# Two-scale attention and two feed-forward layers: the local attention as forty bands of 64 keys, in pairs

## The chip, the cores and the metric

The kernel runs on one core of a Trainium2 chip. The metric is the device time of one execution in microseconds; smaller is better. Engines are named as in the profile: PE (TensorE matmul), PEld (its weight loads), DVE (VectorE), ACT (ScalarE), POOL (GpSimd), SP (SyncE, which issues the DMAs).

## What is computed

Inputs are q, k, v of shape (4, 8, 576, 64): 4 batches, 8 heads, 576 tokens, 64 values a head. All is float32.

```
q_d, k_d, v_d = means of four neighbouring tokens (144 each)
out_up    = repeat(softmax(q_d k_d^T / 8) v_d, 4)
scores    = where(|i - j| < 4, q k^T / 8, -1e9)
out_local = softmax(scores) v
x = (out_up + out_local) as 2304 tokens x 512
h = x @ w_in   (512 x 2048);  x = relu(h)^2 @ w_out   (2048 x 512)
h = x @ w_in2  (512 x 2048);  out = (h * cos(h)) @ w_out2
```

The local attention looks three tokens to either side. In 64 neighbouring tokens a query therefore needs at most 70 keys.

## The kernel before

**Local attention.** A task `window(w)` (L453) works off 64 queries of one batch with their 64 + 6 keys; there are 36 windows, nine a batch. Heads are held in pairs, 128 partitions = 2 heads x 64. For a window PE writes the mask (L478, two bf16 matmuls of 280 columns, in the windows before `W0[3]`; DVE adds it in the later ones, L499), then eight score products (L488, one head each: contraction over 64 partitions, 64 queries x 70 keys, plain float32, all into one PSUM bank). The two heads of a pair use the lower left and the upper right 64 x 64 corner of the array. A softmax follows (`exps`, L359: maximum L360, exponential on ACT L365 or subtraction L372 and L376, sum L378, reciprocal L506, division L507), four transposes (L517, one for each head pair, 70 keys become 70 partitions), a copy out of PSUM on ACT (L519), and eight V products (L537: contraction over 70 keys, 64 x 64). DVE adds the coarse attention (L553) into `xt`, ACT rounds it to `xh` (L564), DVE takes the rest `xl` (L565). In the trace each plain float32 matmul is two MATMUL records.

**Coarse attention.** `pool(b)` (L229) sums four tokens; `down(b, hp)` (L380) is its attention: scores L391, transposes L412, V product L428.

**Feed-forward 1.** Its tokens go in five blocks of 512, 448, 448, 448, 448 (`WINS1`, windows of 64). For each of 16 slices f of the hidden size `stage_a` (L718, 12 matmuls) gives h, ACT makes gt and gh (L746, L747, L734), DVE gl (L740), and `stage_b1` (L800, 12 matmuls) sums into four banks. The weights of slice f come as raw 1 MB loads, and `conv1(f)` with `split` (L586) makes two parts of them: ACT L591, DVE L593, L596, L598, ACT L605 (`hi`), and two subtractions L613 (`loa`, `lob`), on POOL in the first stage and on DVE later.

**Feed-forward 2** (L750, L818) follows without attention.

**Order.** Everything before the first `stage_a` is the first stage (`early`): pooling, the coarse attention of batch 0, the windows of block 0 and `conv1` of slices 0 to 2. After it tasks are advanced once or twice an iteration; `start_at` sets the iteration in which a window, a pool or a conversion begins, `RANK` who goes first, and a scheduler places the instructions of each engine. While block j is multiplied, the windows of block j + 1 are worked off between its matmuls. `need` and `done` count buffers: three PSUM banks `a` serve scores, transposes and V products (in the first stage the banks of `h` and `acc` too).

Of the kernel before, what the change touches and what calls it, by code (L numbers as in the profile page):

```python
# [24 lines left out]
WQ = 64  # L25
WK = WQ + 2 * HALO
NWB = S // WQ
NW = B * NWB
KTOK = SD // 2
# [6 lines left out]
WINS1 = (8, 7, 7, 7, 7)  # L36
# [27 lines left out]
RANK = {"down": 0, "window": 1, "pool": 2, "conv1": 3, "conv2": 3}  # L64


def window_of(w):
    b, i = divmod(w, NWB)
    t0 = i * WQ
    k0, k1 = max(t0 - HALO, 0), min(t0 + WQ + HALO, S)  # L70
    return b, i, t0, k0, k1
# [3 lines left out]
def kernel(  # L75
# [28 lines left out]
    const_sb = const.tile([P, P + WK], F32, name="const_sb")  # L104
    nc.sync.dma_start(out=const_sb, in_=consts)
    ident = const_sb[:, :P]
    const_b = const.tile([P, P + WK], BF16, name="const_b")
# [5 lines left out]
    for t, v in zip(magic, (MAGIC, -MAGIC)):  # L113
# [7 lines left out]
    y_d = [dramp.tile([P, NK, n * WQ], F32, name=f"y_d{j}") for j, n in enumerate(WINS1)]  # L121

    caps = {
        "a": 3, "h": 1, "acc": 4, "qkw": 3, "vw": 3, "pr": 4, "pt": 2, "xt": 2, "qp": 1, "xd": 2, "vp": 1, "av": 3, "pl": 2, "raw": 2,
# [37 lines left out]
    kept = [spare.pop() for _ in range(W0[1] // 2 + 1)]  # L162
# [66 lines left out]
    def pool(b):  # L229
# [8 lines left out]
        for i, hp in parts:  # L238
# [17 lines left out]
            if not early[0]:  # L256
                yield
# [18 lines left out]
    def load_bands():  # L276
        for w in range(0, W0[1], 2):
            t = wp.tile([P, 2 * DM], F32R, tag=f"hi{kept.pop(0)}", name="vband").bitcast(F32)[:WK]
            bands[w], bands[w + 1] = t[:, :DM], t[:, DM:]
            nc.sync.dma_start(  # L280
                out=t.rearrange("p (w c) -> p w c", w=2), in_=win_v[w:w + 2].rearrange("w p c -> p w c")
            )
# [160 lines left out]
    xts = {}  # L443
    placed, added = [0], [0]
# [8 lines left out]
    def window(w):  # L453
        b, i, t0, k0, k1 = window_of(w)
        n, off = k1 - k0, HALO - (t0 - k0)
        apart = early[0]
        if not apart:
            yield from need("qkw")
            qk = cm.tile([P, HPAIR * (WQ + WK)], F32, tag="qkw", name="qkw", bufs=caps["qkw"])
            nc.sync.dma_start(out=qk, in_=win_qk[w])  # L460
            qw = qk[:, :HPAIR * WQ].rearrange("p (h m) -> p h m", h=HPAIR)
            kw = qk[:, HPAIR * WQ:].rearrange("p (h s) -> p h s", h=HPAIR)
        if not apart:
            yield from need("vw")
            vw = cm.tile([WK, DM], F32, tag="vw", name="vw", bufs=caps["vw"])
# [45 lines left out]
        if not early[0]:  # L511
            yield
# [687 lines left out]
```

## Time and profile before

| | us |
|---|---|
| median of 3 runs | 932.44 (931.36 to 932.68) |
| profiled execution | 931.8 |
| its span, first to last instruction | 930.0 |
| PE busy in the span | 907.4 (98%) |
| DVE / ACT / POOL busy | 645.6 / 578.9 / 102.6 |
| DMA bytes | 222.77 MB |

The span is 1.8 us shorter than the execution and both belong to the same run. A matmul of the profile is counted busy until its modelled end, and several lie over one another; so a price for a group of them is better read from where the group and its successor start than from the sum of their durations.

### The profile page before, as it was taken

What the parts mean: (1) busy time and instruction counts of PE and PEld (TensorE: products, weight loads), DVE (VectorE), ACT (ScalarE), POOL (GpSimd) and SP (SyncE); (2) the same over time, 40 slices, a digit from 0 to 9 for tenths busy, and PEclk for the clock granted to TensorE, in tenths of its full rate; (3) what the DMA queues carried; (4) which work ended last, traced back from release to release, by engine and by line L of the source; (5) the groups of instructions that cost most, each with busy time, mean ns of one, the idle gap of its engine ahead of it and who ended that gap; (6) DMA issues with size and microseconds to landing.
All of it is one profiled execution on the core that took longest, in us unless ns stands there. A gap on an engine that the chain in (4) does not pass through costs nothing.

```text
span 930.0 us, 17583 instructions
## 1 busy us (share of the span) xinstructions
PE 907.4 (98%) x6858; PEld 830.1 (89%) x6858; DVE 645.6 (69%) x1231; ACT 578.9 (62%) x1024; POOL 102.6 (11%) x79
## 2 busy tenths in 40 slices
PE   7789999999999999999999999999999999999997
PEld 5668777888889888889899999999999999999997
DVE  6998885663667535646521168879888888879786
ACT  4787774545555455555543377777777776777774
POOL 2111101033033332132110000000000000000000
PEclk9999999999999999999999999999999999999999
DMA  9788876856898677976897876555656666655672
GB/s 230 220 318 299 310 260 205 303 184 221 285 338 290 240 252 250 314 257 231 304 323 248 309 286 199 203 182 197 206 182 196 207 202 194 211 182 196 212 234 102
DMA packets 74223, 222.77 MB, mean 240 GB/s; under 512 B 8932, under 2 KB 14436, under 8 KB 69916
## 3 DMA queue, kind: packets, MB, share of 16 engines
q1 hardware_dynamic: 74140, 221.64, 70.9%
q8 instruction: 54, 0.88, 0.4%
q14 instruction: 29, 0.24, 0.1%
HBM read 180.72 MB, written 40.89 MB: 238 GB/s over the span
## 4 chain that ended last, share of the span: by engine, by line
PE 87%; DVE 6%; DMA 3%; ACT 2%; issue 1%; SPq 0%; POOL 0%; DVEq 0%; ACTq 0%; POOLq 0%
PE ps_h L757 22%; PE ps_h L722 19%; PE acc L805 19%; PE acc L829 18%; DMA pl<-in_pool_v_dram 2%; PE ps_a L537 1%; DMA pl<-in_pool_qk_dram 1%; PE ps_a L488 1%; PE ps_a L517 1%; PE ps_warm L942 1%; PE ps_a L391 1%; PE ps_a L428 1%; PE ps_a L412 1%; PE acc L827 1%; DVE mx L360 1%
## 5 line engine op out<-in xcount | busy, mean ns | idle before, releaser
L757 PE MATMUL ps_h<-x,w2hi 128*128 128x256 f32 x1152 | 159.9, 281 | 0.0
L757 PEld LDWEIGHTS ps_h<-x,w2hi 128*128 128x128 f32 x1152 | 146.6, 189 | 0.1
L829 PE MATMUL acc<-bl,gh 128*128 128x256 f32 x504 | 140.5, 280 | 0.0
L740 DVE TENSOR_TENSOR gl<-gt,gh 128x448 fp32r<-128x448 f32 (+1 forms) x80 | 56.3, 704 | 115.3 <-ACT gh L734 56.2
L722 PE MATMUL ps_h<-xh,w1hi 128*128 128x448 f32 (+1 forms) x320 | 121.4, 381 | 2.8 <-ACT gt L746 1.8
L805 PE MATMUL acc<-gl,w1hi 128*128 128x448 f32 (+1 forms) x320 | 120.8, 377 | 0.2 <-DVE gl L740 0.2
L722 PE MATMUL ps_h<-xl,w1hi 128*128 128x448 f32 (+1 forms) x320 | 119.6, 374 | 0.5 <-DVE xl L565 0.5
L746 ACT ACTIVATE gt<-ps_h 128x448 f32<-128x448 f32 (+1 forms) x80 | 44.2, 552 | 117.3 <-PE ps_h L722 117.0
L805 PE MATMUL acc<-gh,w1hi 128*128 128x448 f32 (+1 forms) x320 | 109.4, 379 | 2.6 <-ACT gh L734 2.6
L829 PEld LDWEIGHTS acc<-bl,gh 128*128 128x128 f32 x504 | 94.9, 188 | 0.0
L805 PE MATMUL acc<-gh,lo 128*128 128x448 f32 x256 | 94.4, 369 | 0.0
L797 DVE TENSOR_TENSOR gl<-g,gh 128x896 fp32r<-128x896 f32 x72 | 78.2, 1086 | 11.0 <-ACT gh L792 11.0
L765 ACT ACTIVATE u<-ps_h,quarter 128x512 f32<-128x512 f32 x72 | 49.4, 686 | 51.4 <-PE ps_h L757 51.2
L829 PE MATMUL acc<-w2hi,gh 128*128 128x256 f32 x288 | 80.9, 281 | 0.0
L829 PE MATMUL acc<-w2hi,gl 128*128 128x256 f32 x288 | 80.3, 281 | 0.0
L772 DVE SCALAR_TENSOR_TENSOR r<-u,ps_h 128x512 f32<-128x512 f32 x72 | 49.4, 687 | 40.2 <-ACT u L767 34.8
L792 ACT ACTIVATE gh<-g 128x896 fp32r<-128x896 f32 x72 | 68.1, 946 | 10.7 <-DVE g L790 10.6
L777 ACT ACTIVATE r<-r,half_pi 128x512 f32<-128x512 f32 x72 | 51.8, 720 | 33.8 <-DVE r L773 33.8
L722 PEld LDWEIGHTS ps_h<-xh,w1hi 128*128 128x128 f32 x320 | 60.1, 188 | 12.0 <-ACT gt L746 3.4
L757 PE MATMUL ps_h<-x,w2lo 128*128 128x256 f32 x432 | 68.7, 281 | 0.0
L805 PEld LDWEIGHTS acc<-gh,w1hi 128*128 128x128 f32 x320 | 59.6, 188 | 10.2 <-ACT gh L734 3.1
L805 PEld LDWEIGHTS acc<-gl,w1hi 128*128 128x128 f32 x320 | 60.7, 190 | 7.0 <-DVE gl L740 0.5
(149 smaller groups left out, 1952.1 us busy)
## 6 DMA issues: line engine op xcount, KB each, us to landing
bl<-wo_d SPq DMA_DIRECT2D x70, 896.0 KB
raw<-in_w_dram SPq DMA_DIRECT2D x32, 1024.0 KB
lo<-lo_d SPq DMA_DIRECT2D x128, 256.0 KB
qkw<-in_win_qk_dram SPq DMA_DIRECT2D x28, 268.0 KB
pl<-in_pool_qk_dram SPq DMA_DIRECT2D x24, 288.0 KB
wo_d<-raw SPq DMA_DIRECT2D x16, 384.0 KB
out_dram<-o SPq DMA_DIRECT2D x18, 256.0 KB
lo_d<-loa SPq DMA_DIRECT2D x16, 256.0 KB
```

Of the source, the lines that this page charges most:

```text
L360: last["max"] = nc.vector.tensor_reduce(out=mx[:, 0], in_=sv, op=ALU.max, axis=AX.X).ins
L722: nc.tensor.matmul(h[:, :n], a[:, c * P:(c + 1) * P], x[:, c, :n], start=i == 0, stop=i == len(order) - 1)
L740: last["gl"] = nc.vector.tensor_tensor(out=gl, in0=gt, in1=gh.bitcast(F32), op=ALU.subtract).ins
L746: last["relu"] = nc.scalar.activation(out=gt, in_=h, func=AF.Relu).ins
L757: nc.tensor.matmul(h[:, s * TB:(s + 1) * TB], a[:, c * P:(c + 1) * P], x[:, c], start=i == 0, stop=i == len(order) - 1,)
L765: nc.scalar.activation(out=u, in_=h, func=AF.Identity, bias=quarter, scale=float(1.0 / (2 * math.pi)))
L772: nc.vector.scalar_tensor_tensor(out=r, in0=u, scalar=-PI2_HI, in1=hv, op0=ALU.mult, op1=ALU.add)
L777: nc.scalar.activation(out=r, in_=r, func=AF.Sin, bias=half_pi, scale=1.0)
L792: nc.scalar.activation(out=gh, in_=g[:, 1:], func=AF.Copy)
L797: nc.vector.tensor_tensor(out=gl, in0=g[:, 1:], in1=gh.bitcast(F32), op=ALU.subtract)
L805: nc.tensor.matmul(acc[d][:, :n], a, x, start=f == 0 and i == 0, stop=f == NF - 1 and i == 2)
L829: nc.tensor.matmul(o, a[:, x], b, start=opens and i == 0, stop=p == NP2 - 1 and i == 2 and (k % 2 == 1 or k == NPROD - 1),)
```

## The change

The 576 tokens of a batch are cut into ten bands of 60, 56 or 58 queries (`WIDTHS`) whose keys are exactly 64. There are 40 bands, eight in each block, and the blocks have 460, 460, 464, 460 and 460 tokens. A task `pair(q)` takes two bands. Scores and V products are 64 x 64 in every dimension: contraction over 64 partitions, 64 stationary columns, 64 (V: 56 to 60) moving columns. The four products that stand next to one another in the source have the four combinations of the lower or upper 64 rows with the left or right 64 columns of the array, and the two row halves write to two different PSUM banks. The order of the products follows: the query half `a` of a head pair picks the rows and the bank, the head pair's index `c` the output partitions; in the V products the key half `g` picks the rows and the bank. One softmax runs for each bank (`soft`), so two for a pair. A transposed piece now has 128 x 128, two for each bank. Masks are written for each corner. The adds of the coarse part are two for a pair.

Beside that: `conv1(0)` holds its three DVE steps back until all first-stage divisions are issued, `conv1(1)` until the first block's input is complete; the first-stage subtractions L613 move from POOL to DVE; `pt` has 5 buffers instead of 2, `qkw` and `vw` 2 larger ones instead of 3; pairs start by a changed table of iterations; `pool` of the last two batches loads one step more slowly.

```
-WQ = 64
-WK = WQ + 2 * HALO
-NWB = S // WQ
+WQ = WK = 64
+WIDTHS = (60, 56, 58, 58, 56, 56, 58, 58, 56, 60)
+NWB = len(WIDTHS)
...
-WINS1 = (8, 7, 7, 7, 7)
+WINS1 = (8,) * 5
...
+    def soft(s, sv, pr_tag, pr, q, a, pts):
...
+        yield from exps(s, sv, mx, pr, SCALE, a == 0 if apart else 2 * q < W0[2])
...
+        for i in range(2):
+            both_g = pr[:, 2 * i:2 * i + 2].rearrange("p g s -> p (g s)")
+            last["pe"] = nc.tensor.transpose(tpv[:, i], both_g, ident).ins
...
-        for hp in range(HPAIR):
-            for rows in halves_of:
...
-                last["pe"] = nc.tensor.matmul(sv[rows, hp], qa, ka, start=by_dve, stop=by_dve or hp == HPAIR - 1).ins
...
+        ss = yield from need_a(2)
...
+        for group in ((0,), (1,)) if at[0] != at[1] else ((0, 1),):
+            cs = slice(2 * group[0], 2 * group[-1] + 2)
+            for c in range(2) if not by_dve else ():
+                for a, rows in enumerate(halves_of):
+                    nc.tensor.matmul(
+                        svs[a][halves_of[c], cs], ident_b[rows, rows],
...
+            for i in group:
+                t0, _, k0 = geo[i]
+                for g in range(2):
+                    for c in range(2):
+                        for a, rows in enumerate(halves_of):
+                            hp = 2 * c + g
...
+                            last["pe"] = nc.tensor.matmul(
+                                svs[a][halves_of[c], 2 * i + g], qa, ka,
...
-        for hp in range(HPAIR):
-            for a in range(2):
-                rows = slice(a * D, (a + 1) * D)
-                last["pe"] = nc.tensor.matmul(
-                    avv[rows, hp], vw[:n, hp * P + a * D:hp * P + (a + 1) * D], pt[:n, hp, a * WQ:(a + 1) * WQ],
...
+        avs = yield from need_a(2)
...
+            for c in range(2):
+                for g in range(2):
+                    keys = slice(g * WK, (g + 1) * WK)
+                    for a in range(2):
+                        v0 = i * HALF + c * P + a * D
+                        last["pe"] = nc.tensor.matmul(
+                            avv[g][a * D:(a + 1) * D, c, off:off + wide], vw[keys, v0:v0 + D],
+                            pts[a][1][keys, i, c * WQ:c * WQ + wide], start=True, stop=True,
...
+        while held_back and held_back():
+            yield
-        with behind("gl", "xl"):
+        with behind("pr" if early[0] and not added[0] else "gl", "xl"):
...
-                eng = nc.gpsimd if early[0] else nc.vector
-                eng.tensor_tensor(out=lo, in0=xv[:, cs], in1=hi[:, cs].bitcast(F32), op=ALU.subtract)
+                nc.vector.tensor_tensor(out=lo, in0=xv[:, cs], in1=hi[:, cs].bitcast(F32), op=ALU.subtract)
...
-    tasks += [conv1(0), conv1(1, 3), conv1(2, 6)]
+    tasks += [pair(q) for q in range(W0[1] // 2)]
+    tasks += [conv1(0), conv1(1, 2), conv1(2, 6)]
...
+        waits = {0: lambda: divided[0] < W0[1], 1: lambda: len(ready) < W0[1]}
+        for said in split(raw, hi1[f], ring, held_back=waits.get(f) if early[0] else None):
...
-        start_at(m if j == 1 else NF * (j - 1) - 7 + 2 * m, window, w)
+        start_at(m if j == 1 else NF * (j - 1) - 9 + 2 * m, pair, q)
```

How the instructions move, on two engines.

PE in blocks 0 and 1, where attention for the next block stands between the matmuls of the feed-forward. `qkw` holds queries and keys, `vw` the values, `pt` the transposed weights of the softmax, and a number behind `ps_a` names one PSUM bank. Before, one window's V products and two windows' masks and scores:

```order
L537 MATMUL ps_a<-pt,vw 64x64 x8
L478 LDWEIGHTS const_b
L478 MATMUL ps_a<-const_b 64x280
L478 LDWEIGHTS const_b
L478 MATMUL ps_a<-const_b 64x280
L488 MATMUL ps_a<-qkw 64x70 x8
L478 LDWEIGHTS const_b
L478 MATMUL ps_a<-const_b 64x280
L478 LDWEIGHTS const_b
L478 MATMUL ps_a<-const_b 64x280
L488 MATMUL ps_a<-qkw 64x70 x8
```

The change, masks (L544) and scores (L561) of one pair; bank 1384 belongs to one half of the rows, bank 1385 to the other:

```order
L544 LDWEIGHTS const_b_89
L544 MATMUL ps_a_1384<-const_b_89 64x256
L544 LDWEIGHTS const_b_89
L544 MATMUL ps_a_1384<-const_b_89 64x256
L561 MATMUL ps_a_1384<-qkw_1286 64x64 x8
L544 LDWEIGHTS const_b_89
L544 MATMUL ps_a_1385<-const_b_89 64x256
L544 LDWEIGHTS const_b_89
L544 MATMUL ps_a_1385<-const_b_89 64x256
L561 MATMUL ps_a_1385<-qkw_1286 64x64 x8
```

And V products (L602) of another pair, the beginning:

```order
L602 MATMUL ps_a_1600<-pt_1122,vw_981 64x60
L602 MATMUL ps_a_1600<-pt_1163,vw_981 64x60
L602 MATMUL ps_a_1601<-pt_1122,vw_981 64x60
L602 MATMUL ps_a_1601<-pt_1163,vw_981 64x60
L602 MATMUL ps_a_1600<-pt_1122,vw_981 64x60
L602 MATMUL ps_a_1600<-pt_1163,vw_981 64x60
L602 MATMUL ps_a_1601<-pt_1122,vw_981 64x60
L602 MATMUL ps_a_1601<-pt_1163,vw_981 64x60
```

The scheduler keeps the order of the source only in part. In the V products shown the banks alternate, so all four corners follow one another; in the scores shown one bank's eight products go first and the other's after them, so only the two column halves of one row half alternate. Over the 16 pairs whose products stand between or just ahead of the feed-forward (256 scores, 256 V products), 120 scores and 140 V products stand in groups of four corners, the other 136 and 116 bank by bank. These attention runs of one kind number 52 in the program before (26 with scores, 26 with V products); in the change scores and V products, which have the same corners, stand in 44 stretches.

DVE at the end of the first stage. `bits` is the conversion of slice 0, `pr` and `mx` the softmax, `xt` and `xl` the input of block 0, `loa` and `lob` the low parts. Before:

```order
L593 TENSOR_SCALAR bits<-bits 128x1024
L505 TENSOR_SCALAR mx<-mx 128x4
L507 TENSOR_TENSOR pr<-pr,mx 128x280
L506 RECIPROCAL mx<-mx 128x4
L378 TENSOR_REDUCE mx<-pr 128x4
L596 TENSOR_SCALAR bits<-bits 128x1024
L506 RECIPROCAL mx<-mx 128x4
L507 TENSOR_TENSOR pr<-pr,mx 128x280
L505 TENSOR_SCALAR mx<-mx 128x4
L598 SCALAR_TENSOR_TENSOR bits<-raw,bits 128x1024
L507 TENSOR_TENSOR pr<-pr,mx 128x280
```

The change:

```order
L491 TENSOR_TENSOR pr<-pr,mx 128x256
L663 TENSOR_SCALAR bits<-bits 128x1024
L666 TENSOR_SCALAR bits<-bits 128x1024
L668 SCALAR_TENSOR_TENSOR bits<-raw,bits 128x1024
L684 TENSOR_TENSOR loa<-bits,w1hi_538 128x512
L684 TENSOR_TENSOR lob<-bits,w1hi_538 128x512
L619 TENSOR_TENSOR xt<-ps_acc,xd 128x2x116 x4
L633 TENSOR_TENSOR xl<-xt,xh 128x4x116
L619 TENSOR_TENSOR xt<-ps_acc,xd 128x2x112 x2
```

The conversion of slice 0 stands behind the last division instead of between the divisions, its two subtractions are on DVE, and all four `xl` of the block follow one another without the conversion of slice 1 between them.

## Rows read from the trace of the kernel before

**Rows 1.** The page, part 1: engine busy us, share of the span, instructions.

```profile
PE 907.4 (98%) x6858; PEld 830.1 (89%) x6858; DVE 645.6 (69%) x1231; ACT 578.9 (62%) x1024; POOL 102.6 (11%) x79
```

**Rows 2.** Busy us by stretch: length, PE, PEld, DVE, ACT, POOL, PEclk, DMA, GB/s.

```profile
56.60:60.00 3.40, 3.40 (x10) 2.62 (x9) 3.29 (x8) 3.39 (x16) 0.96 (x1) 0.50 0.95 301
60.00:100.00 40.00, 40.00 (x239) 31.95 (x239) 37.39 (x71) 31.95 (x76) 6.58 (x6) 1.00 0.88 306
100.00:150.00 50.00, 50.00 (x330) 39.16 (x329) 39.75 (x70) 36.53 (x85) 4.69 (x5) 1.00 0.80 269
150.00:170.00 20.00, 17.81 (x165) 13.86 (x163) 13.34 (x29) 7.07 (x15) 0.65 (x1) 1.00 0.69 218
170.00:430.00 260.00, 258.23 (x1804) 227.50 (x1803) 149.43 (x296) 138.25 (x252) 67.14 (x45) 1.00 0.78 266
```

**Rows 3.** Groups of PE instructions by line after the first stage, busy us, mean ns.

```profile
L488 PE MATMUL ps_a<-qkw 64*64 64x70 f32 (+1 forms) x448 | 18.8, 223 | 0.0
L537 PE MATMUL ps_a<-pt,vw 70*64 70x64 f32 (+1 forms) x448 | 18.6, 226 | 1.0 <-issue 1.0
L517 PE MATMUL ps_a<-const_sb,pr 128*70 128x128 f32 (+1 forms) x112 | 16.9, 273 | 0.8 <-POOL pr L507 0.8
L478 PE MATMUL ps_a<-const_b 64*64 64x280 bf16 (+1 forms) x28 | 4.2, 297 | 0.0
```

**Rows 4.** PE in order of time, block 0: start us, length us, what.

```profile
63.62 0.69 PE L537 MATMUL ps_a<-pt,vw 67*64 67x64 f32 x16
64.24 0.31 PE L478 MATMUL ps_a<-const_b 64*64 64x280 bf16 x2
64.38 0.65 PE L488 MATMUL ps_a<-qkw 64*64 64x70 f32 x16
...
71.58 0.71 PE L488 MATMUL ps_a<-qkw 64*64 64x70 f32 x16
72.22 0.50 PE L805 MATMUL acc<-gh,w1hi 128*128 128x512 f32 x1
```

**Rows 5.** The chain that ended last, on PE in blocks 0 and 1: start us, us.

```profile
60.92 2.77 PE ps_h L722 x12
...
75.26 0.73 PE ps_a L391 x6
...
79.70 0.44 PE ps_a L517 x4
...
171.49 2.44 PE ps_h L722 x12
```

**Rows 6.** Feed-forward 2, for weight loads: the page, part 5, and a stretch of 100 us.

```profile
L757 PEld LDWEIGHTS ps_h<-x,w2hi 128*128 128x128 f32 x1152 | 146.6, 189 | 0.1
...
600.00:700.00 100.00, 100.00 (x842) 99.73 (x841) 84.44 (x155) 72.60 (x103) 0.00 (x0) 1.00 0.59 195
```

**Rows 7.** DVE in order of time at the end of the first stage.

```profile
36.31 0.45 DVE L507 TENSOR_TENSOR pr<-pr,mx 128x280 f32<-128x280 f32 x1
...
37.48 1.28 DVE L553 TENSOR_TENSOR xt<-ps_acc,xd 128x256 f32<-128x256 f32 x3 [0.71 <-ACT xd L436]
...
46.77 0.68 DVE L565 TENSOR_TENSOR xl<-xt,xh 128x512 fp32r<-128x512 f32 x1
...
55.89 0.69 DVE L740 TENSOR_TENSOR gl<-gt,gh 128x512 fp32r<-128x512 f32 x1
```

**Rows 8.** The chain that ended last, first stage.

```profile
35.86 1.06 ACT w1hi L605
...
42.11 0.70 DVE bits L593
...
43.56 1.22 DVE bits L598
...
50.16 1.42 DVE bits L593
```

**Rows 9.** POOL in order of time at 48 us.

```profile
48.50 1.29 POOL L613 TENSOR_TENSOR loa<-bits,w1hi 128x512 fp32r<-128x512 f32 x1 [9.00 <-ACT w1hi L605]
```

More of the change, by code (lines that the diff above doesn't have):

```diff
@@ L63, with first_token, mask_at @@
 PRODUCTS = ((5, 5), (0, 0), (3, 6), (1, 1), (4, 4), (2, 2), (6, 3))
-RANK = {"down": 0, "window": 1, "pool": 2, "conv1": 3, "conv2": 3}
+RANK = {"down": 0, "pair": 1, "pool": 2, "conv1": 3, "conv2": 3}
 def window_of(w):
     b, i = divmod(w, NWB)
-    t0 = i * WQ
-    k0, k1 = max(t0 - HALO, 0), min(t0 + WQ + HALO, S)
-    return b, i, t0, k0, k1
+    t0 = sum(WIDTHS[:i])
+    return b, t0, WIDTHS[i], min(max(t0 - HALO, 0), S - WK)
+def first_token(w):
+    if w == NW:
+        return B * S
+    b, t0, _, _ = window_of(w)
+    return b * S + t0
+def mask_at(w):
+    _, t0, _, k0 = window_of(w)
+    return P + 1 + HALO - (t0 - k0)
+DVE_MASK = W0[3]
+LAG_ONE = True
+T0 = [first_token(w) for w in W0]
+NT = [b - a for a, b in zip(T0, T0[1:])]
 @with_exitstack
@@ L161 @@
     spare = list(range(AHEAD, NF))
-    kept = [spare.pop() for _ in range(W0[1] // 2 + 1)]
+    kept = [spare.pop() for _ in range(W0[1] // 4 + 1)]
     held, taken = {}, {}
@@ L255, in pool @@
                 continue
-            if not early[0]:
-                yield
+            for _ in range(1 if b < 2 else 2):
+                if not early[0]:
+                    yield
             if b < PE_POOLED:
@@ L442 @@
     xblk = {}
-    xts = {}
-    placed, added = [0], [0]
+    placed, added, divided = [0], [0], [0]
     def x_tiles(j):
@@ L458, in window @@
             yield from need("qkw")
[L459 to L465, printed above, removed]
-            nc.sync.dma_start(out=vw, in_=win_v[w])
+            qk = cm.tile([P, 2 * HPAIR * (WQ + WK)], F32, tag="qkw", name="qkw", bufs=caps["qkw"])
+            nc.sync.dma_start(out=qk, in_=win_qk[q])
+            qw = qk[:, :2 * HPAIR * WQ].rearrange("p (w h m) -> p w h m", w=2, h=HPAIR)
+            kw = qk[:, 2 * HPAIR * WQ:].rearrange("p (w h s) -> p w h s", w=2, h=HPAIR)
             yield
@@ L475, in window @@
         halves_of = [slice(a * D, (a + 1) * D) for a in range(2)]
-        by_dve = w >= W0[3]
-        for rows in halves_of if not by_dve else ():
-            nc.tensor.matmul(
-                sv[rows], ident_b[rows, rows], band[rows, off:off + n].unsqueeze(1).broadcast_to([D, HPAIR, n]),
-                start=True, stop=False,
-            )
-        for hp in range(HPAIR):
-            for rows in halves_of:
-                if apart:
-                    qa, ka = whole[0, hp][rows, t0:t0 + WQ], whole[1, hp][rows, k0:k1]
-                else:
-                    qa, ka = qw[rows, hp], kw[rows, hp, :n]
-                last["pe"] = nc.tensor.matmul(sv[rows, hp], qa, ka, start=by_dve, stop=by_dve or hp == HPAIR - 1).ins
+        by_dve = two[0] >= DVE_MASK
@@ L489, in window @@
         if apart:
-            scored.add(w)
+            scored.update(two)
             if len(scored) == W0[1]:
@@ L567, in window @@
             ).ins
-            done("xt")
-        ready.add(w)
+        done("xt")
+        ready.update(two)
     ready = set()
@@ L636, in conv1 @@
             yield
-            while f == 2 and said and early[0]:
+            while f == 2 and said and now[0] < 1:
                 yield
```

221 lines of the change are left out of this document (133 added, 88 removed).

## Prediction

> **What bounds the kernel.** I read the page's busy shares, then the stretches of time, the groups of PE by line, the chain and the timeline. PE is busy for 98% of the span [rows 1], DVE for 69%. From 60 us on PE has almost no gap: 40.00 of 40 us, 50.00 of 50, 17.81 of 20, 258.23 of 260 [rows 2], idle 4.0 us between 60 and 430 us in all. So after the first stage each microsecond taken from PE is a microsecond of the kernel, as long as the others keep up. DVE is the nearest: from 60 to 100 us it works 37.39 of 40 us, and the DMA engines are at 0.88; later DVE falls to 39.75 of 50 and 149.43 of 260 [rows 2]. Before 60 us the order is turned round: DVE leads, and the chain runs through its softmax, adds and conversions to the first feed-forward matmuls [rows 7, 8].
>
> **Scores and V products.** After the first stage there are 448 records each [rows 3], two to a product, eight products a window, so 28 windows. One window's 16 score records start within 0.71 - 0.22 = 0.49 us, and PE goes on to the next matmul 0.64 us after the first (71.58 to 72.22) [rows 4]: 0.49 for the products and 0.15 for leaving the run. What does 70 columns of plain float32 cost alone? Six records of 144 columns over the whole array take 0.73 us [rows 5], 0.85 ns a column; 70 columns would be 59 ns a record and 0.95 us for 16. They took half, so two products do run side by side now. The V records likewise: 0.69 - 0.23 = 0.46 us for 16 [rows 4] where 64 x 0.85 x 16 is 0.87. I call two or more products side by side a pass: a window has four score passes of 0.122 us and four V passes of 0.115 us.
>
> In the change a pass has 64 score columns (0.122 x 64/70 = 0.112 us) or on average 57.5 V columns (0.101 us). With four corners in a pass 16 pairs would need 64 passes for each kind. The order doesn't give that: 120 scores and 140 V products stand in fours, 30 and 35 passes; the other 136 and 116 stand bank by bank, in twos, 68 and 58 passes. Twos that share the rows and differ in columns are what the V products are today, so their price is on record. For fours no row exists. Ends: nothing hinders (0.112 and 0.101, the price of a two), or they go one after another (four times that). I take the first, since records of two corners start 2 to a pass in both arrangements seen, other rows with other columns (scores) and the same rows with other columns (V).
> - Scores: 28 x 4 x 0.122 = 13.7 to 98 x 0.112 = 11.0 us.
> - V products: 28 x 4 x 0.115 = 12.9 to 93 x 0.101 = 9.4 us.
> - Leaving a run: 52 x 0.15 = 7.8 to 44 x 0.15 = 6.6 us.
>
> Together -7.4 us. The scores of two windows, or of one pair, fall just before the feed-forward, which takes about 0.4 of it back: **-7.0**. If fours were as slow as two twos, 65 more passes, +6.9; one after another, three times that.
>
> **Transposes.** 112 after the first stage [rows 3], four in 0.44 us on the chain [rows 5], 0.11 each for 128 moving columns: 12.3 us. The change has 64 with the same 128 columns: 7.0. Their stationary side grows from 70 to 128 columns; a 128 x 128 weight load of 189 ns hides behind matmuls that start every 100/842 us = 0.119 us [rows 6], so I add nothing (at most 64 x 0.01). **-5.3.**
>
> **Masks.** 64.24 to 64.38, 0.14 us a window [rows 4], 12 of them: 28 records [rows 3] are 14 windows, two of which lie ahead of the feed-forward. 1.7 us become about 7 x 0.16. **-0.6.**
>
> **Block sizes.** 12 matmuls take 2.77 us at 512 columns and 2.44 at 448 [rows 5], 0.43 ns a column each. Block 0 has 52 columns less, the others 52 more together; the 36 matmuls of block 0 that lie in the first stage gain outside this sum. **+0.8.**
>
> **First stage.** The last division starts at 36.31, the adds at 37.48, the last `xl` at 46.77, the first gl at 55.89 [rows 7].
> - The conversion of slice 0 (about 2.5 us on DVE: the same three steps for slice 1 take 42.11 to 44.78 with their gaps [rows 8]) moves from between the divisions to behind them. Softmax on 256 instead of 280 columns saves some 28 x 0.025 = 0.7. Divisions end near 33.6, the conversion near 36.1, ACT's `hi` 1.06 us later [rows 8]; then two subtractions on DVE, 2 x 0.6, since POOL no longer does them; the adds begin near 38.4, 0.9 us later than now. Behind the waiting conversion stand, on DVE, only those adds, and on ACT the copies of the coarse part that the adds need; PE's V products don't wait for it.
> - Behind that the conversion of slice 1 no longer stands between the low parts. Eight adds of 0.33 and four `xl` of 0.55 are 4.8 us, plus 1 us of waits for ACT: block 0 is complete near 44.2 instead of 47.4.
> - Then the conversions of slices 1 and 2 (2 x 2.4), two pool sums (1.3), two subtractions (1.2) and small ones: gl near 52.7 instead of 56.5. Today DVE loses time here while POOL subtracts (48.50, 1.29 us each [rows 9]): a step of 0.70 us takes 1.42 [rows 8]. That goes.
> - From 56.6 to 60.0 PE's granted clock is 0.50 [rows 2], 1.2 of 2.4 GHz, after gaps in its first matmuls. A shorter gap may spare that, about 1.7 us.
>
> I take -3.8 and -1.7: **-5.5**; ends -2.0 (the clock falls again, ACT is late) and -7.0.
>
> **Cover of block 0.** What hides DVE's conversions is PE's work, and that shrinks: in 60 to 100 us some 35 us of 512-column matmuls lose a tenth, 3.5 us, and PE starts 5 us earlier on them. DVE's 37.39 us there stay. So PE will wait for weights now and then until about 100 us; afterwards DVE has 10 us to spare in 50. **+2**, ends 0 and +10. POOL's divisions are about as many elements as before (32 x 256 for 28 x 280 columns); DMA bytes hardly change. SP's queue: a pair loads what two windows loaded, in half the issues. The gaps of 4.0 us I leave as they are.
>
> **Sum:** -7.0 - 5.3 - 0.6 + 0.8 - 5.5 + 2 = -15.6 us. 931.8 of the profiled execution becomes 916.2; the median of the runs stands 0.6 above that execution, so **917**.
>
> **Rivals.**
> 1. Fours are no faster than twos: +6.9, 924. For it: the fastest runs shown start 16 records in 0.46 and 0.49 us, about 30 ns a record [rows 4], and a four asks for half that. Against: the two corners seen in each arrangement don't disturb each other. The Trainium skill ("TensorE: Matmul & The Clock Gate", section "Wait — 56ns, not 53.3ns?") says that matmuls never start closer than about 25 ns; by that rule a four, eight records, would need 0.20 us instead of 0.11, and as an estimate from that page, 65 fours x 0.095 us more, the time would be about 923. A mean of 30 ns neither shows nor refutes it. This rival has 15%.
> 2. **Slower:** the two row halves, which now write to two banks through the same columns, exclude each other, and a four goes one product after another: 0.45 and 0.40 us instead of 0.112 and 0.101. 30 x 0.34 + 35 x 0.30 = +20.7, 937. It decides from 0.24 us more a four: there the whole gain is gone. Against it: no arrangement in the trace behaves so. 6%.
> 3. DVE and the raw loads bound block 0: 10 us of waits instead of 2, 925. For it 37.39 of 40 and the DMA share 0.88 [rows 2]. 12%.
> 4. Banks: a pair takes two of the three banks `a` for scores and again for V products, so PE may stand before a bank that DVE has not emptied. 12 pairs in blocks 1 to 3 at one DVE step of 0.6 us: +7, 924. 10%.
> 5. The fours work and the first stage gains 7, no waits: 912, inside the forecast's own spread.
>
> **Numbers.** The forecast 917 has 55% with rival 5. The range 905 to 926 holds it with its ends and rivals 1, 3 and 4; outside lie rival 2, two of these rivals at once, and a still better course. A measurement of this kernel tells apart about 0.2%, 1.9 us: faster 0.92, same 0.02, slower 0.06.
>
> **What would show it.** Runs of V products in fours should start 16 products (32 records) within 0.45 us or so, runs bank by bank in 0.85. The transposes number 64. The first gl comes near 52.7 us; from 60 us PE is busy all the time but for 2 us in block 0, with DVE the releaser. From the end of block 3 on nothing changes but the block's length. I am wrong if fours start as slowly as twos, if PE's idle time after 60 us grows beyond 10 us, or if the first gl comes after 54.5 us.

## The result, and the profile after

The changed kernel takes **920.54 us** (median of 4 runs, 919.69 to 920.82) and the kernel before 931.9 (4 runs): ratio 0.9877, 95% interval 0.986 to 0.9894. Forecast were 917 and a range of 905 to 926. The direction and the range held; 3.5 us of the forecast gain are missing. The profiled execution took 919.69 us, its span is 917.6.

The page after, its parts 1 and 4 (engine busy us, share, instructions; the chain that ended last by engine), answers to [rows 1]:

```profile
PE 896.5 (98%) x6946; PEld 817.6 (89%) x6946; DVE 650.1 (71%) x1266; ACT 572.7 (62%) x1039; POOL 99.1 (11%) x79
...
PE 83%; DMA 7%; DVE 7%; ACT 2%; issue 1%; DVEq 0%; ACTq 0%; SPq 0%
```

PE is still the busiest engine, with 10.9 us less work. The stretches of time (columns as in [rows 2]):

```profile
46.40:50.00 3.60, 2.01 (x8) 1.15 (x6) 3.60 (x6) 2.15 (x5) 0.00 (x0) 0.68 0.35 73
50.00:56.00 6.00, 5.71 (x26) 4.85 (x27) 5.31 (x12) 5.34 (x15) 0.00 (x0) 1.00 1.01 380
...
60.00:100.00 40.00, 38.90 (x293) 32.97 (x292) 37.64 (x75) 32.32 (x94) 8.06 (x7) 1.00 0.94 331
100.00:150.00 50.00, 49.28 (x435) 40.63 (x434) 44.58 (x87) 37.48 (x86) 7.62 (x6) 1.00 0.84 290
150.00:170.00 20.00, 20.00 (x187) 17.37 (x187) 13.25 (x32) 10.04 (x20) 1.80 (x3) 1.00 0.90 303
...
260.00:264.00 4.00, 1.85 (x10) 1.33 (x8) 1.99 (x5) 0.91 (x3) 0.00 (x0) 0.97 1.03 379
264.00:268.00 4.00, 4.00 (x12) 3.50 (x13) 2.32 (x8) 2.96 (x5) 1.58 (x2) 0.60 1.01 297
```

PE loses 1.1 us between 60 and 100 us and 0.7 up to 150, as expected of block 0, nothing between 150 and 260, and then 2.15 us at once, after which its granted clock is 0.60 for 4 us (part of it at 1.2 GHz instead of 2.4).

PE in order of time (start us, us): V products in fours, then eight V products of one bank.

```profile
129.73 0.69 PE L602 MATMUL ps_a<-pt,vw 64*64 64x60 f32 x32
130.34 0.48 PE L794 MATMUL ps_h<-xh,w1hi 128*128 128x460 f32 x1
...
132.85 0.68 PE L602 MATMUL ps_a<-pt,vw 64*64 64x58 f32 x16
133.46 0.48 PE L794 MATMUL ps_h<-xh,loa 128*128 128x460 f32 x1
```

32 records in fours and 16 in twos both take 0.61 us to the next matmul. Before, 16 took 0.62 (V products) and 0.64 (scores) [rows 4].

Where the gain is. I put the time from the start of one matmul to the start of the next down to the line of the first, and call a pause idle where it outlasts the modelled end by more than 20 ns; the account runs from the third group of `stage_a` to the first matmul of feed-forward 2.

| us | before | after | measured | forecast |
|---|---|---|---|---|
| third `stage_a` starts at | 60.68 | 55.54 | -5.1 | -5.5 |
| scores and V products | 32.4 | 26.4 | -6.0 | -7.0 |
| transposes | 11.0 | 6.3 | -4.7 | -5.3 |
| masks | 1.8 | 1.6 | -0.2 | -0.6 |
| coarse attention | 22.3 | 21.9 | -0.3 | 0 |
| feed-forward 1 | 400.9 | 405.1 | +4.2 | +0.8 |
| idle | 4.0 | 4.1 | +0.2 | +2 |
| feed-forward 2 and the edges | | | -0.4 | 0 |
| span | 930.0 | 917.6 | -12.4 | -15.6 |

Of the +4.2, 0.8 are the block sizes: matmuls start 208.8 ns apart in block 0 where they started 232.3 (336 of them, -7.9 us), and 5.3, 7.6, 5.1 and 4.6 ns further apart in the four others (384 each, +8.7). 1.6 are the clock after the gap at 262 us: eight matmuls from 263.97 us on are followed by the next after 0.37 to 0.55 us, 1.57 more in all than at 0.21. The rest, about 1.8, fits 13 more changes from the feed-forward to attention (93 instead of 80), each some 0.05 us on the way in and 0.1 on the way back; no run shows it by itself.

The gap at 262 us, DVE, ACT and PE in order of time (with the idle time before and its releaser):

```profile
257.86 0.63 DVE L812 TENSOR_TENSOR gl<-gt,gh 128x464 fp32r<-128x464 f32 x1
262.01 0.68 DVE L375 TENSOR_REDUCE vp<-pl 72x128 f32<-72x512 f32 x1 [3.52 <-DMA pl<-in_pool_v_dram]
262.62 0.41 DVE L393 TENSOR_TENSOR pr<-pr,mx 128x256 f32<-128x256 f32 x1
...
263.06 0.42 ACT L397 ACTIVATE pr<-pr 128x256 f32<-128x256 f32 x1 [4.67 <-DVE pr L393]
263.38 0.54 ACT L818 ACTIVATE gt<-ps_h 128x464 f32<-128x464 f32 x1
...
263.97 0.76 PE L794 MATMUL ps_h<-xh,w1hi 128*128 128x464 f32 x1 [2.15 <-ACT gt L818]
```

A sum of the coarse part (`vp`) waits on DVE for a load of 144 KB, the softmax subtraction stands behind it, ACT's exponential waits for that, and `gt`, which empties PE's bank `h`, stands behind the exponential. The instructions of this row take 0.4 to 0.8 us each; the time is lost because what stands behind the waiting sum on DVE, and behind the waiting exponential on ACT, starts only after it. The chain shows the load itself:

```profile
253.70 8.29 DMA pl<-in_pool_v_dram
261.99 0.02 issue
262.01 0.68 DVE vp L375
```

### The profile page after: what moved, and what is told of

Read it like the earlier page. It is cut to its first block, busy times and chain, and to the rows that moved or that the text cites. A ratio compares the mean times of both kernels' runs of the same rounds, so it can differ in the third digit from the quotient of the medians.

```text
span 917.6 us, 17798 instructions
## 1 busy us (share of the span) xinstructions
PE 896.5 (98%) x6946; PEld 817.6 (89%) x6946; DVE 650.1 (71%) x1266; ACT 572.7 (62%) x1039; POOL 99.1 (11%) x79
## 4 chain that ended last, share of the span: by engine, by line
PE 83%; DMA 7%; DVE 7%; ACT 2%; issue 1%; DVEq 0%; ACTq 0%; SPq 0%
PE ps_h L829 22%; PE acc L901 19%; PE acc L877 17%; PE ps_h L794 17%; DMA raw<-in_w_dram 3%; DMA pl<-in_pool_qk_dram 1%; DVE bits L668 1%; PE ps_warm L1014 1%; DMA pl<-in_pool_v_dram 1%; PE ps_a L602 1%; PE ps_a L561 1%; DMA lo<-lo_d 1%; ACT bits L659 1%; PE acc L899 1%; PE ps_a L412 1%
## 5 line engine op out<-in xcount | busy, mean ns | idle before, releaser
L812 DVE TENSOR_TENSOR gl<-gt,gh 128x460 fp32r<-128x460 f32 (+1 forms) x80 | 58.7, 734 | 130.9 <-ACT gh L806 68.5
L794 PE MATMUL ps_h<-xh,w1hi 128*128 128x460 f32 (+1 forms) x320 | 122.5, 385 | 7.1 <-ACT gt L818 4.0
L877 PE MATMUL acc<-gl,w1hi 128*128 128x460 f32 (+1 forms) x320 | 120.7, 377 | 0.1
L794 PE MATMUL ps_h<-xl,w1hi 128*128 128x460 f32 (+1 forms) x320 | 120.2, 377 | 0.0
L818 ACT ACTIVATE gt<-ps_h 128x460 f32<-128x460 f32 (+1 forms) x80 | 44.1, 552 | 119.6 <-PE ps_h L794 119.4
L877 PE MATMUL acc<-gh,w1hi 128*128 128x460 f32 (+1 forms) x320 | 111.6, 379 | 0.4 <-ACT gh L806 0.4
L877 PE MATMUL acc<-gh,lo 128*128 128x460 f32 (+1 forms) x256 | 95.4, 373 | 0.0
L794 PEld LDWEIGHTS ps_h<-xl,w1hi 128*128 128x128 f32 x320 | 60.9, 190 | 6.6 <-issue 0.4
```

Source lines behind the costliest of these rows:

```text
L794: nc.tensor.matmul(h[:, :n], a[:, c * P:(c + 1) * P], x[:, c, :n], start=i == 0, stop=i == len(order) - 1)
L812: last["gl"] = nc.vector.tensor_tensor(out=gl, in0=gt, in1=gh.bitcast(F32), op=ALU.subtract).ins
L818: last["relu"] = nc.scalar.activation(out=gt, in_=h, func=AF.Relu).ins
L877: nc.tensor.matmul(acc[d][:, :n], a, x, start=f == 0 and i == 0, stop=f == NF - 1 and i == 2)
```

## The experiments

Ratios are to the kernel before, in runs on the same chip. Groups of runs come from different chips, so between two versions the ratios are the fairer comparison. Idle times and prices are counted as in the table above, from one profiled execution each.

**e1: all products in fours.** Short diff:

```
+    tc.add_manual_dep(ins, chain[-1].name, NoSync, ...)   # every score and V product of a pair
-                for g in range(2):
+                for g in (1, 0):
...
-                    for a in range(2):
+                    for a in (1, 0):
```

> The changed kernel with the order of the products written down: within a pair each score and each V product is chained behind the one before it, so that four successive products always take four different corners (in the V products the second key half and the second query half come first, because their operands are the last to be ready). In the changed kernel 136 of the 256 scores and 116 of the 256 V products behind the first stage run bank by bank, in twos. Theory (a four costs what a two costs): its trace shows a pair's 32 score records with the way back to the feed-forward in 0.625 us in fours and 1.154 us (0.666 + 0.488) bank by bank, V 0.618 against 1.214 us; 8.5 pairs of scores x 0.53 + 7.25 pairs of V x 0.60 = 8.9 us less, and some six runs fewer at 0.25 us. Against it stands that a four can start only when both banks and both transposed weights are there. I expect 912 us (909 to 916). Rival (fours gain nothing): 920, within 1 us. Rival (a pair that waits for two banks at once stops PE): 918 or more, with PE idle behind 60 us above 10 us.

Measured: 933.09 us, ratio 1.0014 (1.0 to 1.0028). A clear miss. The products did fall, to 22.3 us, but the third `stage_a` came at 63.33 us, and PE idled 12.1 us after it. In the first stage PE's granted clock is 0.50 from 22 to 56.1 us. The waits of PE behind 60 us, longest first:

```profile
PE ps_a L503 <- POOL pr L491: 3.4, 3, 1.9
PE ps_a L614 <- DMA vw<-in_win_v_dram: 3.1, 1, 3.1
```

So the price fell and the waits grew; how much of the waits comes from the late first stage is not told by this run. e5 tells it.

**e2: all products bank by bank**, the bank outermost in both loops, and chained as in e1.

> The changed kernel with all products bank by bank: the loops over the bank are outermost and each product is chained behind the one before it, so that only two corners with the same rows alternate. 120 scores and 140 V products that stood in fours now stand in twos. Theory (a four costs what a two costs): 7.5 pairs of scores x 0.53 + 8.75 pairs of V x 0.60 = 9.2 us more, 929 to 930 us, almost the time of the kernel before; the transposes and the first stage then carry what is left. Rival (fours gain nothing): 920 to 921.

Measured: 923.53 us, ratio 0.9903 (0.9883 to 0.9924). The products cost 29.0 us, 2.6 more than in the changed kernel, where 9.2 was expected: a miss by size. The first stage was late here too (third `stage_a` at 59.84), idle time 2.8 us.

**e5 and e6: the same two orders behind the first stage alone** (in e5 the chain of e1, in e6 that of e2, both with `if chain and not early[0]`).

> As e1_fours, but the order is written down only behind the first stage, which stays as in the changed kernel (in e1_fours the third group of stage_a came at 63.33 instead of 55.54 us). By e1_fours the price of the products falls by 4.1 us against the changed kernel (scores 13.20 to 11.25, V products 13.18 to some 11.0), because the trace has 32 V records in fours with the way back in 0.618 us, the same in twos in one piece in 0.896, and only two pieces of 16 in 2 x 0.607; and PE's idle time behind 55 us grew from 4.1 to 12.1 us. Theory (the price falls, the waits give it back): third group of stage_a at 55.5, products -4, waits +4 to +8, 920 to 925 us. Rival (the waits of e1_fours came from its late first stage): waits as in the changed kernel, 916 to 917 us.

> As e2_twos, but the order is written down only behind the first stage. Theory (a pass of two and a pass of four cost the same 0.07 us): 65 passes more are 4 to 5 us of PE time less what longer runs save; e2_twos showed 2.4 us. With the first stage of the changed kernel (third group of stage_a at 55.5 instead of 59.84 us) and waits between 3 and 6 us: 919 to 924 us. Rival (fours gain nothing): products within 0.5 us of the changed kernel's 26.4 us.

Measured: e5 923.8 us, ratio 0.99 (0.988 to 0.992); e6 922.88, ratio 0.9897 (0.9863 to 0.9931). Neither is faster than the changed kernel (0.9877). In e5 the products fell by 3.7 us and the idle time rose by 6.6, with the first stage as in the changed kernel: the waits come with the order. In e6 the products cost 3.0 us more than in the changed kernel, a little less than the 4 to 5 expected.

**e7: the same corner next to itself**: the order is bank, output half, then the four products of that corner, chained behind the first stage.

> Behind the first stage products that stand next to each other take the same corner: four of the first corner, four of the second, and so on, chained. This measures a product without a neighbour in another corner. Theory (products run side by side only in different corners, a product alone takes 64 columns x 2 records x 0.85 ns = 0.109 us, a price taken from the whole-array records of before): 32 records of a pair take 16 x 0.109 + 0.3 = 2.0 us instead of 0.62 in fours, 32 pieces x 1.4 = 45 us more, 965 us. Rival (a 64 x 64 product runs at 0.42 ns a column by itself): 32 records in 16 x 0.054 + 0.3 = 1.2 us, 18 us more, 938 us. Rival (side by side is nothing, the records follow each other anyway): 0.9 us as in twos.

Measured: 934.22 us, a single run. The products cost 44.2 us, 17.8 more than in the changed kernel, where the theory had 45: a miss. The number is that of the first rival, but its mechanism (0.054 us a product) isn't there, as the start times show. PE in order of time, one pair's 32 V records and the matmul behind them, in fours (e5), twos (e6) and ones (e7):

```profile
352.72 0.69 PE L611 MATMUL ps_a<-pt,vw 64*64 64x60 f32 x32
353.34 0.48 PE L886 MATMUL acc<-gl,w1hi 128*128 128x464 f32 x1
```

```profile
400.17 0.97 PE L611 MATMUL ps_a<-pt,vw 64*64 64x56 f32 x32
401.06 0.48 PE L803 MATMUL ps_h<-xh,w1hi 128*128 128x460 f32 x1
```

```profile
410.11 1.51 PE L611 MATMUL ps_a<-pt,vw 64*64 64x56 f32 x32
411.55 0.48 PE L803 MATMUL ps_h<-xh,w1hi 128*128 128x460 f32 x1
```

0.62, 0.89 and 1.44 us for the same work. The start times of the single records say why. In the fours of e5 three starts follow at 7 ns and the first record of the next round comes after 38: a round of 58 ns. In the V products before, and in the pieces of 16, two records start 7 ns apart and the next two 51 later: again 58. In e7 successive records of one corner start 58 or 59 ns apart. **One round takes 58 to 59 ns whether it holds one, two or four records**, so a pass (two rounds) takes 0.117 us, not the 0.07 of e6's expectation. (Only the first round of a run is longer, about 105 ns, and the next matmul starts 148 ns after the last record.) Twos in one piece come out below 16 rounds, and ones below 32, because where the corner changes the next corner's records already start beside the last ones (pairs 14 and 44 ns apart in e7).

The ladder, from the profiled execution of each kernel; "stretch" is the time from the third `stage_a` to the first matmul of feed-forward 2:

| kernel | products, us | idle, us | third `stage_a` | stretch, us | median, us |
|---|---|---|---|---|---|
| e7, ones | 44.2 | 0.8 | 56.86 | 478.7 | 934.2 (one run) |
| before | 32.4 | 4.0 | 60.68 | 472.3 | 931.9 |
| e6, twos | 29.4 | 4.6 | 57.00 | 467.9 | 922.9 |
| changed | 26.4 | 4.1 | 55.54 | 465.5 | 920.5 |
| e12, scores in fours | 24.5 | 5.0 | 55.01 | 463.7 | 920.6 |
| e5, fours | 22.7 | 10.7 | 55.35 | 468.7 | 923.8 |

The kernel before differs in more than its products; from e7 to e6 and on to the changed kernel, 14.8 and 3.0 us of products are 10.7 and 2.5 us of the stretch. (The medians of e6 and the changed kernel lie within each other's noise.) All in twos, the products already cost 3.0 us less than before, although there are more of them (992 records against 864); the fours that the scheduler leaves give the other 3.0 of the 6.0. With all products in fours, what leaves PE's work comes back as its waits, and more. Those of e5 behind 55 us:

```profile
PE ps_h L803 <- ACT gt L827: 4.0, 5, 2.1
PE ps_a L611 <- DVE xt L628: 2.2, 1, 2.2
PE ps_h L803 <- ACT w1hi L686: 2.1, 2, 1.7
PE acc L886 <- ACT y L924: 1.3, 1, 1.3
PE ps_a L555 <- DVE xt L628: 1.0, 1, 1.0
```

3.2 us of them are products and masks that wait for a bank which DVE's add has not emptied yet.

**e12: only the scores in fours**, V products free.

> The half of e5 that leaves the V products alone: only the scores behind the first stage are chained in fours, the V products stand as the scheduler likes. In e5 the products fell by 3.7 us (scores 13.20 to 11.53, V products 13.18 to 11.13) and PE's idle time rose by 6.6 us; its two longest waits inside attention were V products before a load of values (2.24 us at 169 us) and masks before a bank (0.98 us). Theory (a fixed order of the V products makes the waits, because they need both transposed weights, the values and two banks at once): scores -1.7 us, idle time within 2 us of the changed kernel's 4.1, 918 to 920 us: at or a little below the changed kernel. Rival (any fixed order costs more waiting than it spares, since the waits come from loads and in-order queues elsewhere, and shift with every schedule): 921 to 926 us, idle time 6 us or more.

Measured: 920.57 us (917.13 to 921.04), ratio 0.9874 (0.9858 to 0.9891): the changed kernel's time. The profiled execution is the 917.13 one and has no gap at 262 us; the three others lie at 920.5 to 921.0, so its idle time of 5.0 us need not be theirs. (The expectation put the 2.24 us wait in e5 down to a load; the rows of e5 above name DVE's add, so a bank.) The scores fell by 1.0 us, not 1.7, and the V products by 0.9 without being fixed. Fixing the scores alone does avoid most of e5's waits, and gains nothing that can be measured: the stretch is 1.7 us shorter in that one fastest execution. No version was found that is measurably faster than the changed kernel.

**e3: the sums of the coarse part later** (`range(1 if b < 2 else 3)` instead of `2`).

> The changed kernel with one step more between the loads of the coarse part of batches 2 and 3 and the DVE sums that read them. In its trace PE stands still once behind 150 us for long, 2.15 us from 261.8 on, and its clock is 0.60 from 264 to 268 us after that. Theory: DVE waits there 3.5 us for a load of values (vp L375) that was issued 8.3 us before, the softmax subtraction L393 stands behind it, ACT's exponential L397 waits for that, and gt L818 stands behind the exponential. With the sum later in DVE's queue the wait is gone: 3 to 4 us less, 917 us, and no PE gap over 1 us between 230 and 300 us. Rival (the gap is one of PE's own banks or of a late weight): 920, the gap stays.

Measured: 924.56 us, ratio 0.9907 (0.9891 to 0.9923), slower than the changed kernel where 3 to 4 us less were expected. The gap at 262 us is gone, as the theory has it; between 230 and 300 us the waits of PE are now

```profile
PE ps_a L602 <- DMA vw<-in_win_v_dram: 0.7, 1, 0.7
```

but another has come, at 366 us:

```profile
368.99 0.75 PE L877 MATMUL acc<-gh,w1hi 128*128 128x460 f32 x1 [2.79 <-ACT y L915]
```

Here ACT's copy of a block's result waits 3.3 us for a store (`wo_d<-raw`). Scores and V products cost 2.4 us more, too, in more pieces (42 runs of scores and 30 of V products instead of 37 and 26).

**e11: the last coarse part two iterations earlier** (`(3, 26)` for `(3, 28)`), and **e10: three `pl` buffers** (`"pl": 3`, `"pt": 3`).

> The changed kernel with the coarse part of the last batch started two iterations earlier (at 26 instead of 28), so that its loads of values come before the store of a block's result (920 KB) and not beside it. Theory (the gap at 262 us is those loads landing late): the loads land in 6 us or less, no gap over 1 us between 230 and 300 us, 917 us. Rival (each shift of the schedule moves such a gap to another place, as in e3, where it went from 262 to 366 us): 919 to 925 us with another gap of 2 us or more.

> The changed kernel with three buffers instead of two for the coarse part's loads (pl), and three instead of five for the transposed weights (pt) to make room. The 2.15 us gap of the changed kernel at 262 us, and its like in e4 (3.29 us), e5 (2.09) and e8 (2.85) between 262 and 287 us, is a DVE sum that waits for a load of values which could be issued only when the sum before had freed its buffer, some 8.3 us before it landed. Theory: with a third buffer the load is issued one sum earlier, the wait shrinks below what PE's queued work covers, no gap over 1 us between 230 and 300 us: 3 to 4 us less, 917 us, if pt needs no more than three. Rival (three pt buffers hold the pairs up): PE waits for transposes, 922 or more. Rival (the DMA engines are full there, an earlier issue only makes the load longer): gap stays, 920.

Measured: e11 922.28 us, ratio 0.9895 (0.9848 to 0.9942); e10 925.88, ratio 0.993 (0.9907 to 0.9954). In e11 the first load of values is issued at 242.29 instead of 253.70 us, and DVE waits 0.92 us for it instead of 3.52:

```profile
247.51 0.68 DVE L375 TENSOR_REDUCE vp<-pl 72x128 f32<-72x512 f32 x1 [0.92 <-DMA pl<-in_pool_v_dram]
```

But the fifth load of the batch, issued at 256.37, is now the slow one, and PE's wait of 2.3 us is before a transpose (the load and the sum, then PE's waits from 230 to 300 us):

```profile
256.37 8.96 DMA pl<-in_pool_v_dram
265.33 0.02 issue
265.35 0.69 DVE vp L375
```

```profile
PE ps_a L503 <- POOL pr L491: 2.3, 1, 2.3
```

So the long wait stays near the same time and changes the load that it hits. In both kernels the slow load is issued behind the same group: a raw 1 MB load, two loads `lo` and one of `vw`, and a store of 512 KB, all issued within the 3 us before it; two cases don't show that this is the cause. The reason that the expectation gave is out: in the changed kernel the store of the block's result is issued 5 us after the slow load has landed.

```profile
266.98 0.32 SPq L918 DMA_DIRECT2D y_d<-y  x1
```

In e10 DVE waits longer for the loads (6.8 us between 230 and 300 us) without a PE wait over 0.3 us there, but PE idles 10.1 us, most of it in blocks 0 and 1; whether that is the third `pl` buffer or the lost `pt` buffers was not separated. The DMA engines' share at the gap is 1.03 and 1.01 of full in the changed kernel.

**e4: nothing held back in the first stage** (`held_back=None`, `conv1(1, 3)`, and `behind("gl", "xl")` as before).

> The changed kernel without the holding back in the first stage: the DVE steps of the conversion of slices 0 and 1 start as soon as their load is there, as in the kernel before; the first-stage subtractions stay on DVE. Theory (the holding back is worth most of what the first stage gains): DVE does the 2.4 us of slice 0 between the divisions and those of slice 1 between the low parts, so the input of block 0 is complete some 3 us later, the third group of stage_a starts near 58.5 instead of 55.5 us, and the time is 923 to 924 us. Rival (the subtractions moved off POOL made the gain): third group of stage_a within 1 us of 55.5, 920 to 921 us.

Measured: 932.76 us, ratio 1.0002 (0.9985 to 1.0019): 12 us lost, where 3 were expected. The third `stage_a` comes at 61.12, 5.6 us later. The reason is another than the theory's. PE in order of time, e4 and then the changed kernel:

```profile
35.29 1.54 PE L503 MATMUL ps_acc<-const_sb,pr 128*128 128x128 f32 x6 [2.50 <-DVE pr L491]
...
37.62 4.11 PE L449 MATMUL ps_acc<-dpt,vp 72*64 72x144 f32 x32
41.66 3.92 PE L602 MATMUL ps_acc<-pt,vband 64*64 64x60 f32 x128
```

```profile
33.16 1.05 PE L503 MATMUL ps_acc<-const_sb,pr 128*128 128x128 f32 x6 [1.01 <-DVE pr L491]
...
34.57 2.18 PE L449 MATMUL ps_acc<-dpt,vp 72*64 72x144 f32 x32
37.55 3.06 PE L602 MATMUL ps_acc<-pt,vband 64*64 64x60 f32 x128 [0.80 <-ACT xd L457]
```

With the conversion between the divisions PE stands 2.50 us instead of 1.01, and from then on its granted clock is 0.50 up to 45.3 us (1.2 of 2.4 GHz; in the changed kernel it is 1.00 from 34 to 42 us):

```profile
35.10:45.30 10.20, 10.01 (x166) 8.67 (x168) 4.09 (x11) 4.52 (x11) 0.00 (x0) 0.50 0.46 157
```

The same 32 and 128 records then take 8.0 us for 5.2, and DVE, which was to be kept busy, waits 5.65 us for them. The other half of the 12 us lies behind: idle time is 8.7 us instead of 4.1, 5.1 of it between 61 and 107 us and 3.3 in a gap at 273 us that ends with the same sum of the coarse part. How the holding back of the first stage would spare these is not shown.

**e9: the first-stage subtractions back on POOL.**

> The changed kernel with one part of the first stage undone: the two subtractions of each slice's low part run on POOL in the first stage, as before; the holding back stays. e4 showed that without the holding back the third group of stage_a comes at 61.1 instead of 55.5 us. Theory (the two work together: POOL's subtraction slows DVE's step beside it from 0.70 to 1.42 us, and the first feed-forward matmuls wait for the low parts): third group of stage_a 1 to 3 us later, 922 to 924 us. Rival (the holding back alone is the gain): third group of stage_a within 0.5 us of 55.5, 920 to 921 us.

Measured: 922.25 us, ratio 0.988 (0.9848 to 0.9912), third `stage_a` at 57.40. That looks like the theory, but of the eight kernels whose first stage is written as in the changed one, three have their third `stage_a` at 54.99 to 55.35 and five at 56.86 to 58.51. The clock goes with it: e11, at 57.98, has a pause of 2.90 us before its second group and then matmuls 0.38 us apart up to 55 us; the changed kernel, at 55.54, has its slow stretch from 46.4 to 50 us (0.68), where PE waits anyway. So e9 settles nothing about what POOL is worth. Its trace does show the slowing itself: beside POOL's subtractions (49.40 to 52.88 us) DVE's step L668 takes 1.94 us, where it takes 1.21 in the changed kernel.

**e8: each transpose twice.**

> The changed kernel with each of the 64 transposes behind the first stage written twice, one behind the other into the same place. It prices a transpose in its place and tells whether PE's time there is the kernel's. Theory (0.1 us each, all on the path): 64 x 0.1 = +6.4, 927 us if the waits stay as they are; PE's idle time may shrink by up to 2 us since every other engine gets that time. Rival (a 128-column transpose hides beside its neighbour): +1 or less, 921 us.

Measured: 927.83 us (924.16 to 930.86), ratio 0.9938 (0.9918 to 0.9958). The transposes' share of PE's time rose from 6.3 to 13.6 us, 0.114 us for each added one, and the stretch from the third `stage_a` to feed-forward 2 by 8.2 us. As expected: PE's time at this place is the kernel's time. The time of the whole kernel tells it less exactly: the median rose by 7.3 us, by the ratios to the kernel before it is 5.7, and the profiled execution has its third `stage_a` 3.0 us later.

## Why the prediction was right, and where it was not

**Right: what bounds.** After the first stage PE's time is the kernel's (e8: +7.3 of transposes, +8.2 from the third `stage_a` to feed-forward 2). That holds for work added; taken away beyond the changed kernel, it comes back as waits (e5). The main terms have the right sign and order.

**Right: a four costs what a two costs.** Rival 1 is out, and with it the bound that stood beside it: the Trainium skill ("TensorE: Matmul & The Clock Gate", section "Wait — 56ns, not 53.3ns?") says that matmuls never start closer than about 25 ns. Here records of different corners start 7 ns apart, and eight records take 0.117 us, not 0.20. The section does not speak of corners; for them these runs decide. The forecast held that a mean of 30 ns neither shows nor refutes the bound. The single records of the kernel before already refute it: in the runs of [rows 4] the two records of a pair start 3 to 7 ns apart and the next pair 51 ns or more later. Rival 2 (one after another) is out by the same start times.

**Right in the number, not in the form: scores and V products**, -6.0 instead of -7.0. The forecast took a pass in proportion to its columns, "0.122 x 64/70 = 0.112 us" and 0.101 for V. The round is 58 to 59 ns for 56 to 64 columns alike, so a pass is 0.117: 98 x 0.005 + 93 x 0.016 = 2.0 us too little. Twos in one piece, cheaper than 16 rounds, gave some of it back, how much was not measured. And "52 x 0.15 to 44 x 0.15" counted only stretches with scores and V products; with transposes, which now come two by two, and the coarse part, PE changes 93 times instead of 80. At about 0.15 us each that would be the +1.8 that is left in the feed-forward.

**Transposes and masks**: -4.7 for -5.3, mostly because four of the 112 transposes before stand ahead of the third `stage_a` and so outside the account (108 to 64), and a little because a transpose costs 0.10 and not 0.11; -0.2 for -0.6, because 40 mask records stand there instead of 24: each corner has its own, and a pair whose two bands need different masks writes them twice.

**First stage**: -5.1 for -5.5, and the steps come as forecast. DVE in the changed kernel:

```profile
38.58 1.31 DVE L619 TENSOR_TENSOR xt<-ps_acc,xd 128x232 f32<-128x232 f32 x4
...
42.82 1.38 DVE L633 TENSOR_TENSOR xl<-xt,xh 128x448 fp32r<-128x448 f32 x2
...
52.06 0.63 DVE L812 TENSOR_TENSOR gl<-gt,gh 128x460 fp32r<-128x460 f32 x1
```

The adds begin at 38.58 (forecast 38.4), the block is complete at 44.2 (44.2), and the first `gl` starts 3.8 us earlier than before (3.8; the forecast's 52.7 stands against 56.5 and so is the end of `gl`, which comes at 52.7). The fall of the clock is not spared, it has moved: from 56.6 to 60 us before, to 45.3 to 48.7 us now, where PE waits anyway; the third `stage_a` gains 1.3 us more than `gl` (forecast 1.7). What the forecast did not see: undone in the changed kernel, the holding back costs by another way, the PE pause of 2.50 us and the slow clock that followed it (e4). The kernel before had no slow clock in that place:

```profile
33.00:56.00 23.00, 17.64 (x245) 13.96 (x244) 20.02 (x38) 13.85 (x27) 5.03 (x4) 1.00 0.72 248
```

And where the next fall of the clock lies decides 2 us more (e11). With third `stage_a` anywhere from 55.0 to 58.5 us in kernels that share this first stage, that the term came out so near is in part luck.

**Block 0**: +2 for waits; measured 1.8 us of idle time between 60 and 150 us. But the releaser is not DVE alone. The longest, 1.1 us before 97.3, begins at a raw load:

```profile
ACT bits L659 <- DMA raw<-in_w_dram: 3.2, 1, 3.2
...
PE ps_h L794 <- ACT w1hi L677: 1.1, 1, 1.1
```

That is rival 3's "raw loads", at a tenth of its 10 us of waits.

**The step that failed**: "The gaps of 4.0 us I leave as they are." The idle time did stay at 4.1, but it is not the same idle time: before, 2.8 of it lay at 158 to 171 us and the clock held; now 2.15 us lie in one piece at 262 us, and the slow clock behind it costs 1.6 more. That the sum is the same is luck. Rival 4 (banks) didn't show in the changed kernel (0.2 us). It does in e5, where every product needs two banks at once: 3.2 us. Rival 5's 912 does not follow from its own terms, 917 less 1.5 and 2; that would be 913.5. It did not come.

So the missing 3.2 us of the span are, from the table: products 1.0, transposes 0.6, masks 0.4, first stage 0.4, and 1.6 for the clock and 1.8 for changes in the feed-forward, against 1.8 of waits that did not come and 0.7 elsewhere.

**What stays open**: why the wait for the last coarse loads reaches PE so differently. The same row of releasers (load, `vp`, `pr`, `gt`) stands behind a gap of 0.5 us in the kernel before, of 2.1 to 3.3 us in the changed kernel, e4, e5, e8 and e9, and of none over 0.3 us in the profiled e12, though DVE waits for these loads there too. In e2 and e6 DVE waits 6 us for such a load, and PE's longest wait there is 0.9 and 1.3 us. The step that the change itself adds to these loads (`range(1 if b < 2 else 2)`) was not undone alone, nor were the larger buffers for the pairs (`pt`, `qkw`, `vw`), nor was POOL's part in the first stage settled. Whether all fours without the waits of e5 are to be had was not tried; e3, e10 and e11 tried three ways against the gap at 262 us, and none made the kernel faster.

## What to carry to other kernels

Products on different corners of the array cost nothing beside each other here (58 to 59 ns a round for one, two or four), and a scheduler's order decides whether they meet; but look at what feeds them before forcing that order, since a group that needs two banks and two operands at once waits for the later of each. When the bounding engine has been relieved by some per cent, its waits become the kernel's time, and in this kernel they came down rows of engines that keep their order: an instruction that waits for a load holds up everything behind it on its engine, and through that a third engine. Price a pause of PE with the clock that follows it: in the first stage of e4 a pause 1.5 us longer went with 5.6 us of delay, and the 2.15 us at 262 us cost 3.7 with the slow matmuls behind them.

## What the runs showed of the hardware that was not expected

- A round of 64 x 64 float32 records takes 58 to 59 ns for 56 to 64 columns, and for one to four corners (after, e5, e7); the forecast had 0.85 ns a column.
- Records of different corners also run side by side where the order doesn't alternate them: 16 V products in twos, one bank after the other, took 0.89 us in one piece and 2 x 0.61 in two. Part of that is one way in and back less; 16 full rounds with one way in and back would be about 1.08 us, an estimate from 58.5 ns a round, 105 for the first and 148 to the next matmul.
- In e4 the granted clock was 0.50 from 35.1 to 45.3 us although PE was busy 10.01 of 10.20 us there; a pause of 2.5 us lay before. In e1 it was 0.50 from 22 to 56.1 us, with PE busy 28.3 of 34.1.
